# Scratch of q and k in DRAM by head pair, with loads split by head parity

## The chip, the cores and the metric

One NeuronCore of a Trainium2 chip runs the whole kernel. The metric is the device time of one execution in microseconds (us). Most executions of a kernel agree to 0.3%, some are 1 to 2% longer.

## The reference

Eight batches (B = 8) of causal attention with H = 8 heads of D = 64 over S = 576 tokens, each head with 16 extra "beacon" keys in front, then an MLP (512 to 2048 to 512, ELU) on all 4608 tokens:

```python
k_all = concat([beacon_k, k], axis=2); v_all = concat([beacon_v, v], axis=2)
scores = q @ k_all^T / sqrt(64), causal over k
attn = softmax(scores) @ v_all                # (8, 8, 576, 64)
x = attn.transpose(0, 2, 1, 3).reshape(4608, 512)
out = elu(x @ w_in) @ w_out                   # fp32
```

## The kernel before

TensorE needs q and k with d on the partitions. Batches 0 and 1 are transposed on TensorE. For batches 2 to 7, POOL (the GpSimd engine) issues loads that cast q and k from fp32 to bf16 into a DRAM scratch (four loads a tensor, each 144 tokens of all heads), and SP (SyncE) issues DMA transposes out of the scratch, two (q and k) for each head pair:

```python
    @step
    def ld(b, i, s0):                       # issued by POOL; i = 0: q, 1: k; s0 = 0, 144, 288, 432
        if (b, i) not in st:
            st[b, i] = dram.tile([S, H, D], BF16, tag=f"qk{i}", name="qkd")
        s1 = s0 + S // 4
        nc.gpsimd.dma_start(
            out=st[b, i][s0:s1], in_=(q, k)[i][b, :, s0:s1].rearrange("h s d -> s h d"))

    @step
    def ct(b, p):                           # issued by SP, one head pair p
        for i in range(2):
            nc.sync.dma_start_transpose(
                out=keys(b, p)[:, i, NB:SK], in_=st[b, i][:, 2 * p:2 * p + 2, :].rearrange("s h d -> s (h d)"))
    # ... cut: scores, exp, masks, sums, MLP
```

The order of all steps is a fixed list of words. A word "ld.3.0.144:a.1.3.3" is the load of batch 3, q, tokens from 144, held back ("gated") until the named step is done. The score matmuls S read `keys(b, p)`; TensorE's instructions stand in this order too, so a late transpose stops what is behind it (in the changed kernel once for 17.4 us).

The softmax here doesn't subtract the row's maximum and nothing guards it: scores larger than these inputs give would overflow.

## Time and profile before

| | before |
|---|---|
| time, median (range) | 344.25 us (343.25 to 348.1, 4 runs) |
| profiled execution | 342.8 us, granted TensorE clock 0.996 |
| TensorE busy / idle | 328.5 / 14.3 us |
| last load of batches 2 / 4 / 7 landed at | 54.6 / 106.9 / 187.5 us |
| median distance between landings of q/k loads | 1.5 us |

The main views are in the prediction below. Here are the lines of the transfers (DMA view of the kernel before: total packets; then tensors, issuing queue, count, KB each, median us from issue to landing):

```profile
DMA packets 137536, 35.97 MB, mean 105 GB/s; under 512 B 125712, under 2 KB 132880, under 8 KB 137488
...
qkd<-in_q_dram POOLq DMA_DIRECT2D x24, 144.0 KB, 5.7
qkd<-in_k_dram POOLq DMA_DIRECT2D x24, 144.0 KB, 5.6
...
qk<-qkd SPq DMA_TRANSPOSE x48, 4.9
```

and POOL's time on the loads (its groups of instructions: count | busy us, mean ns of one | idle before):

```profile
L174 POOL DMA_DIRECT2D qkd<-in_k_dram x24 | 22.0, 919 | 11.9 <-DVE ls L480 4.1 <-DVE et L378 2.8 <-DVE qk L282 2.2
```

At the median a load lands within 6 us, and a transpose takes 4.9 us.

### The profile page before, as it was taken

How to read it: one execution, taken by the hardware profiler on the slowest of the kernel's cores; microseconds unless marked ns; L12 is line 12 of the kernel's file. 1: busy time of each engine (PE TensorE's matmuls, PEld its weight loads, DVE VectorE, ACT ScalarE, POOL GpSimd, SP SyncE). 2: the span in 40 equal slices, each digit the busy share in tenths (PEclk: the TensorE clock that was granted, in tenths of full speed). 3: DMA queues.
4: the chain of work that ended last, by engine and by line, in shares of the span. 5: the costliest groups of instructions: out<-in, count | busy, mean ns of one | idle time of the engine just before them, and what ended most of it. 6: DMA issues, size and time to landing. Idle time of an engine off the chain costs nothing.

```text
span 342.8 us, 10834 instructions
## 1 busy us (share of the span) xinstructions
PE 328.5 (96%) x4694; PEld 187.0 (55%) x4694; DVE 252.0 (74%) x583; ACT 209.3 (61%) x250; POOL 98.2 (29%) x126
## 2 busy tenths in 40 slices
PE   7989999889999999999999999999999999999992
PEld 3656786355555555565555565555455555555551
DVE  1668599599999999788999987798876456783000
ACT  1988962788795876898796688735424225242111
POOL 7485456554174445342253001200000000000000
PEclk9999999999999999999999999999999999999998
DMA  8999999999999999999999644411000013003104
GB/s 127 159 152 184 205 173 148 140 144 110 174 113 147 119 218 129 149 145 112 167 123 106 105 143 29 32 13 65 0 2 2 0 63 122 3 2 122 63 0 185
DMA packets 137536, 35.97 MB, mean 105 GB/s; under 512 B 125712, under 2 KB 132880, under 8 KB 137488
## 3 DMA queue, kind: packets, MB, share of 16 engines
q0 software_dynamic: 102240, 18.49, 70.0%
q1 hardware_dynamic: 34528, 16.39, 24.1%
q8 instruction: 37, 0.61, 0.8%
q10 hardware_dynamic: 720, 0.39, 0.4%
q14 instruction: 11, 0.09, 0.1%
HBM read 37.22 MB, written 16.52 MB: 157 GB/s over the span
## 4 chain that ended last, share of the span: by engine, by line
PE 83%; DVE 6%; DMA 6%; ACT 2%; issue 1%; POOL 0%; SPq 0%; DVEq 0%; ACTq 0%; POOLq 0%
PE ops L601 35%; PE hps L560 32%; PE sc L325 6%; PE ut L391 4%; DVE gt L585 3%; DMA qk<-qkd 2%; DMA w_in<-in_moe_w_in_dram 2%; PE lt L391 2%; DVE gt L578 1%; PE lt L496 1%; PE tqk L274 1%; DMA stg<-in_q_dram 1%; DVE qk L293 1%; DMA out_dram<-osb 1%; PE ua L391 1%
## 5 line engine op out<-in xcount | busy, mean ns | idle before, releaser
L560 PE MATMUL hps<-xT,w_in 64*128 64x512 f16 (+1 forms) x1280 | 140.0, 355 | 2.4 <-DVE xT L451 1.2
L601 PE MATMUL ops<-w_out,gt 64*128 64x512 f16 x1152 | 138.2, 376 | 0.0
L362 ACT ACTIVATE et<-sc 128x1024 f16<-128x1024 f32 (+4 forms) x128 | 104.6, 867 | 21.9 <-PE sc L325 20.5
L573 ACT ACTIVATE e<-hps 128x1024 f32<-128x1024 f32 x72 | 73.2, 1023 | 62.6 <-PE hps L560 59.9
L560 PEld LDWEIGHTS <-w_in 64*128 64x128 f16 x1280 | 68.4, 94 | 52.7 <-issue 2.5
L601 PEld LDWEIGHTS <-gt 64*128 64x128 f16 x1152 | 62.9, 94 | 53.6 <-issue 0.3
L585 DVE TENSOR_TENSOR gt<-hps,gt 128x1024 f16<-128x1024 f32 x72 | 87.8, 1221 | 4.7 <-DVE gt L578 0.5
L578 DVE TENSOR_SCALAR gt<-e 128x1024 f16<-128x1024 f32 x72 | 49.8, 694 | 21.3 <-ACT e L573 21.0
L191 POOL DMA_DIRECT2D v<-in_v_dram x40 | 33.8, 849 | 62.7 <-DVE xT L451 22.6
L378 DVE TENSOR_TENSOR et<-et,triu 128x256 f16<-128x256 f16 (+6 forms) x185 | 38.0, 253 | 10.0 <-ACT et L362 9.9
L325 PE MATMUL sc<-qk 64*128 64x64 bf16 (+16 forms) x528 | 39.1, 247 | 1.6 <-DMA qk<-qkd 1.5
L325 PEld LDWEIGHTS <-qk 64*128 64x128 bf16 x528 | 23.1, 94 | 18.1 <-DMA qk<-qkd 2.2
L480 DVE TENSOR_TENSOR ls<-ls,et 128x672 f16<-128x672 f16 (+2 forms) x84 | 29.4, 366 | 0.6
L174 POOL DMA_DIRECT2D qkd<-in_q_dram x24 | 21.4, 899 | 27.2 <-DVE qk L282 9.7
L614 ACT COPY osb<-ops 128x1024 f32<-128x1024 f32 x11 | 11.1, 1011 | 25.1 <-PE ops L601 25.1
L391 PEld LDWEIGHTS <-v 128*32 128x32 f16 x1248 | 21.0, 96 | 8.1 <-issue 2.4
L174 POOL DMA_DIRECT2D qkd<-in_k_dram x24 | 22.0, 919 | 11.9 <-DVE ls L480 4.1
L451 DVE TENSOR_TENSOR xT<-ut,rl 128x448 f16<-128x448 f32 (+6 forms) x56 | 20.0, 413 | 2.9 <-PE ut L391 1.9
L391 PE MATMUL ut<-et,v 128*32 128x512 f16 (+4 forms) x560 | 19.0, 278 | 0.0
L630 DVE COPY osb<-ops 128x512 f32<-128x512 f32 x1 | 0.7, 692 | 24.6 <-PE ops L601 24.6
L480 DVE TENSOR_TENSOR ls<-et 128x928 f16<-128x928 f16 x28 | 17.5, 634 | 0.3
L525 ACT ACTIVATE rl<-lt 128x576 f32<-128x576 f32 x14 | 9.1, 653 | 9.3 <-PE lt L391 9.3
(47 smaller groups left out, 122.1 us busy)
## 6 DMA issues: line engine op xcount, KB each, us to landing
out_dram<-osb SPq DMA_DIRECT2D x17, 512.0 KB, 3.5
qkd<-in_q_dram POOLq DMA_DIRECT2D x24, 144.0 KB, 5.7
qkd<-in_k_dram POOLq DMA_DIRECT2D x24, 144.0 KB, 5.6
v<-in_v_dram POOLq DMA_DIRECT2D x24, 128.0 KB, 4.9
w_in<-in_moe_w_in_dram POOLq DMA_DIRECT2D x8, 256.0 KB, 8.5
w_out<-in_moe_w_out_dram POOLq DMA_DIRECT2D x4, 512.0 KB, 9.4
v<-in_v_dram POOLq DMA_DIRECT2D x8, 112.0 KB, 4.1
stg<-in_k_dram POOLq DMA_DIRECT2D x3, 288.0 KB, 5.9
```

The lines of the kernel that those rows point to most:

```text
L174: nc.gpsimd.dma_start(out=st[b, i][s0:s1], in_=(q, k)[i][b, :, s0:s1].rearrange("h s d -> s h d"))
L191: nc.gpsimd.dma_start(out=v_tile(b)[r0:r0 + n_, j, :, :], in_=v[b, :, ilo[j]:ilo[j] + n_, :].rearrange("h s d -> s h d"))
L325: nc.tensor.matmul(out=s[:, h, o0 + a - c0:o0 + e - c0], lhsT=t[D * h:D * (h + 1), 1, P * j:P * (j + 1)], rhs=t[D * h:D * (h + 1), 0, NB + ...
L362: nc.scalar.activation(out=ets[b, p][:, :, c0:c1], in_=s[:, :, o0:o0 + c1 - c0], func=AFT.Exp, bias=0.0, scale=SCALE)
L378: nc.vector.tensor_tensor(out=o, in0=o, in1=triu[0:kc[j], :, t0:t0 + e - a], op=ALU.mult)
L391: nc.tensor.matmul(out=t[32 * i:32 * (i + 1), a - qa:e - qa], lhsT=ones[0:kc[j], :] if half is None else v16[0:kc[j], j, h, half::2], rhs= ...
L480: nc.vector.tensor_tensor(out=lsum[b, p][0:kc[j], :, qj - q1:], in0=in0, in1=e_[0:kc[j], :, cj:cj + S - qj], op=ALU.add)
L560: both.append(nc.tensor.matmul(out=hp[t, i][:, out_, w * u:w * (u + 1)], lhsT=w_in16[rows, cc, P * fc:P * (fc + 1)], rhs=xt[k_][rows, cc, ...
L573: nc.scalar.activation(out=eb[t, i], in_=hp[t, i], func=AFT.Exp, bias=0.0, scale=1.0)
L578: nc.vector.tensor_scalar(out=rb[t, i], in0=eb[t, i], scalar1=1.0, scalar2=1.0, op0=ALU.min, op1=ALU.subtract)
L585: nc.vector.tensor_tensor(out=gt, in0=hp[t, i], in1=gt, op=ALU.max)
L601: both.append(nc.tensor.matmul(out=o_[out_][:, 0, :] if len(o_) == 2 else o_[0][:, out_, :], lhsT=gts[t, fc][rows, P * (2 * tp + out_):P * ...
```

## The change

Intent: in the old scratch a transpose reads 576 rows of 256 B, one every 1024 B. With the scratch laid out as [head pair, token, parity, d], it reads one contiguous block of 147 KB. A load of all heads would then need a pattern of four dimensions (pair, token, parity, d); to stay at three, each load takes 288 tokens of the four even or the four odd heads.

```diff
     def ld(b, i, s0):
         if (b, i) not in st:
-            st[b, i] = dram.tile([S, H, D], BF16, tag=f"qk{i}", name="qkd")
-        s1 = s0 + S // 4
+            st[b, i] = dram.tile([NP, S, 2, D], BF16, tag=f"qk{i}", name="qkd")
+        s0, e_ = s0 // (S // 2) * (S // 2), s0 // (S // 4) % 2
+        s1 = s0 + S // 2
         nc.gpsimd.dma_start(
-            out=st[b, i][s0:s1], in_=(q, k)[i][b, :, s0:s1].rearrange("h s d -> s h d"))
+            out=st[b, i][:, s0:s1, e_, :], in_=(q, k)[i][b].rearrange("(p e) s d -> p e s d", e=2)[:, e_, s0:s1, :])
 ...
     def ct(b, p):
         for i in range(2):
             nc.sync.dma_start_transpose(
-                out=keys(b, p)[:, i, NB:SK], in_=st[b, i][:, 2 * p:2 * p + 2, :].rearrange("s h d -> s (h d)"))
+                out=keys(b, p)[:, i, NB:SK], in_=st[b, i][p].rearrange("s e d -> s (e d)"))
```

## The prediction

> **What bounds the kernel now.** I read the busy totals first, then the slices, the waits, and last the timeline where a wait names the tiles that the change touches.
>
> ```profile
> span 342.8 us, 10834 instructions
> PE 328.5 (96%) x4694; PEld 187.0 (55%) x4694; DVE 252.0 (74%) x583; ACT 209.3 (61%) x250; POOL 98.2 (29%) x126
> ...
> PE   7989999889999999999999999999999999999992
> ...
> DMA  8999999999999999999999644411000013003104
> ...
> q0 software_dynamic: 102240, 18.49, 70.0%
> q1 hardware_dynamic: 34528, 16.39, 24.1%
> ```
>
> TensorE has work in 328.5 of 342.8 us; only 14.3 us of its time is idle, most of it in the first eighth. The DMA row is at 9 through slice 22 (to about 195 us), so transfers could also be a limit there. The waits of TensorE (its matmuls, PE, and its weight loads, PEld) from 55 us to the end say whether they are:
>
> ```profile
> PE sc L325 <- DMA qk<-qkd: 1.5, 2, 1.2
> PE hps L560 <- DVE xT L451: 1.2, 1, 1.2
> ...
> PEld L325 <- DMA qk<-qkd: 2.2, 2, 1.7
> ```
>
> The score matmuls (L325) waited for transposed q and k twice, 1.5 us in all on the matmul row. The timeline places both in batch 2, the first batch that takes the DRAM path:
>
> ```profile
> 60.72 0.39 PE L325 MATMUL sc<-qk 64*128 64x512 bf16 x2 [0.31 <-DMA qk<-qkd]
> ...
> 66.14 0.63 PE L325 MATMUL sc<-qk 64*128 64x144 bf16 x12 [1.19 <-DMA qk<-qkd]
> ```
>
> After that TensorE has no gap in most windows (22.00 busy of 22.00 us from 91 to 113, 28.00 of 28.00 from 169 to 197). So the kernel is TensorE-bound, and the q/k path costs 1.5 us today. What the change can win is at most about that; what it can lose is a q/k path that becomes late.
>
> How late may it become? For each batch I took from the trace when its eight loads landed (the 16th count of their semaphores), when the transposes landed, and when the first score matmul of that head pair started. The smallest distance from landing to use over the four pairs is: batch 2: 0.0 us (both waits above), batch 3: 1.8, batch 4: 2.4, batch 5: 3.4, batch 6: 4.8, batch 7: 3.6 us. A delay larger than this stalls TensorE by the excess.
>
> **What the Trainium skill says.** Three places of the page "DMA: Bandwidth & Descriptors" bear on it.
> (1) Section "Why a DMA increments its semaphore by 16 and not by 1": the number k of DMA engines that one transfer uses is the largest number up to 16 that divides the slowest dimension of both access patterns; a software-generated DMA with k below 16 takes k consecutive engines from a round-robin cursor. It also names an exception, in which some such DMAs are cut into ceil(rows/16) rows an engine. The kernel before has no DMA with k under 16 (outer sizes 1152/144, 128, 112, 96, 80, 16), so its trace can't confirm it.
> (2) Section "Why small descriptors are slow (HBM only)": a 256-byte descriptor takes 11 cycles of the DMA engine[...]: from 107 to 109 us the loads ran flat out with 2,418 packets of 128 B (256 B read as fp32), 16 x 2,000 / 2,418 = 13.2 ns each.
> (3) Section "Latency and other measured facts": a DMA transpose reaches 261 GB/s from a non-contiguous source and 350 to 400 from a contiguous one. In the trace a transpose (147 KB, 576 packets of 256 B) alone has its packets within about 1 us, 147 GB/s, and lands 2.7 to 2.9 us after its issue, so neither figure is reached.
>
> **The change part by part.** Instruction counts and order on all engines are unchanged: 48 loads on POOL, 48 transposes on SP, and TensorE, DVE and ACT see the same tiles. Two things change.
>
> Loads. Before, the destination is one run of 1152 rows of 128 B and the source is 144 x 8 rows: both outer sizes divide by 16, so 16 engines get 72 rows each. After, both patterns are 4 (head pairs) x 288 x 64; the slowest dimension is 4, so k = 4 and each engine gets 288 rows. Bytes and descriptors (1152) are the same. Alone, the stream takes 288 x 13.2 ns = 3.8 us in place of 72 x 13.2 = 0.95: a load lands 2.85 us later. The load issued at 91.9 us with empty queues landed at 95.8, 3.9 us; I expect about 6.7 for such a one. As the four consecutive engines rotate, four successive loads cover all 16, and the total work of an engine per batch (2 x 288 against 8 x 72 rows) is the same: throughput stays, latency grows. In a queue that is already backed up even the latency of the last load doesn't grow: an engine has then skipped the three loads between, and finishes the same 2 x 288 = 8 x 72 rows.
>
> That is the case in batch 2: its loads were issued from 24.3 to 48.0 us behind the weights, and the last landed at 54.6, 6.6 us after its issue. So I expect 0 to 1 us there, not 2.85. In batches 3 to 7 the last load was issued with a shorter queue and landed 4.1 to 6.4 us after issue; there I take the full 2.85 us. It passes through the transposes (the first k transpose of each of these batches is issued within 0.3 us of the last k load's landing when SP is free, as in batch 3: 80.9, 81.0) to the first uses.
>
> Transposes. The 576 rows of 256 B become one 147 KB block. TensorE sees only landing times. The skill's ratio, 261 to about 375, applied to the 1 us of packets gives an estimate of 0.3 us less; issue on SP (1.2 us each, median) and the completion stay. Under competing loads it may be more: the second transpose of pair 1 in batch 2 took 7.4 us to land.
>
> Sum on TensorE: batch 2: 0 to +1, less 0.3 to 0.6 of its 1.5 us of waits: about 0. Batch 3: 2.85 - 0.3 - 1.8 = +0.75. Batch 4: 2.85 - 0.3 - 2.4 = +0.15. Batches 5 to 7 have 3.4 us or more: 0. I add 0.5 for loads of v, which use all 16 engines and now end with the slowest group (they landed 15 us or more before use in batches 2 and 3). Total about +1.4 us on the 344.12 us median: **345.5 us**.
>
> **Rivals.**
> A. *The transposes become much faster and the batch-2 waits go.* For: the waits on qk are the only visible cost of this path. Against: they are 1.5 us on the matmul row. Time 342 to 343 us, still within 2%.
> B. *k = 16 stays* (the exception of (1), or a generator that cuts the inner dimension). Then only the transposes change: 343.5 to 344.
> C. *k = 4, but always on the same four engines* (the exception of (1) with one row on each of the first four). Then all 48 loads queue on four engines: 8 x 3.8 = 30 us a batch, plus their share of v (288 rows x 13.2 = 3.8) and of transposes (4608/16 x 13.2 = 3.8), 38 us a batch, where the loads of successive batches now follow at 23 to 31 us. From 24 us on, with about 10 us of weights in front, the last loads end near 24 + 10 + 6 x 38 = 262 us in place of 187.5, and what TensorE still has to do after batch 7's first use (146 us) comes after it: 400 to 425 us. Against: the page gives the rotating cursor as the general case. Nothing in the trace before excludes C. I give it 15%.
> D. *k = 4 rotating, but no backlog helps batch 2 and transposes gain nothing*: +2.85 + 1.05 + 0.45 = 4.4 us, 348.5, plus some for v: 350.
>
> **Range and chances.** A, B and the main line lie between 342 and 347, D at 348 to 350. The three runs before spread from 343.25 to 348.1 by themselves. 342 to 352 holds this, and leaves out C. Faster by 2% would need 6.9 us from a wait of 1.5: 0.02. Slower by 2% is C and a part of worse collisions: 0.19. Same: 0.79.
>
> **What would show it.** Right: loads of q and k land 2.5 to 3 us later after issue where queues are short (the median of 5.6 to 5.7 us becomes 7.5 to 9), the packets of a lone load run at about 300 per us in place of 1,200; transposes land a little sooner than 4.9 us; the waits of L325 for qk grow from 1.5 us to 2 to 4 us, in batches 2 to 4; TensorE's busy time stays near 328.5 us. Wrong: unchanged load landings (B); waits of 10 us and more for qk in every batch and loads landing tens of us after issue (C); or transposes that get slower, as the only new cost that I see no reason for.

## The result, and the profile after

Median 459.45 us (456.62 to 461.35, 4 runs), 33% slower: ratio 1.331, 95% interval 1.318 to 1.344. A ratio here is the mean time of one kernel's fast runs over that of the other's in the same rounds, so not quite the ratio of the medians quoted. The forecast of 342 to 352 us was wrong.

The same views of the changed kernel. Its page, busy totals, slices (PE, granted clock PEclk, DMA) and software queue:

```profile
span 456.4 us, 10834 instructions
...
PE 349.2 (77%) x4694; PEld 189.7 (42%) x4694; DVE 262.2 (57%) x583; ACT 210.6 (46%) x250; POOL 141.9 (31%) x126
...
PE   8887908588319914994299559809999999999994
...
PEclk9998967799859975998589859967999999999998
DMA  9999999999999999999999999965341000120213
...
DMA packets 303424, 36.63 MB, mean 80 GB/s; under 512 B 291600, under 2 KB 298768, under 8 KB 303376
...
q0 software_dynamic: 268128, 19.15, 87.1%
```

The instruction counts are the same to the last one, the span is 113.6 us longer. TensorE's idle time grew from 14.3 to 107.2 us and its busy time by 20.7 us; the clock row dips in and after the slices where it stood still (0.884 on average, 0.996 before), so I take most of the 20.7 for a result of the stops and not a cause. From slice 28 of the 40 on the PE row is as before.

What TensorE waited for (waits of the changed kernel: us in total, times, longest):

```profile
PEld L326 <- DMA qk<-qkd: 78.4, 9, 17.9
PE sc L326 <- DMA qk<-qkd: 73.8, 9, 17.4
...
PE ops L602 <- DMA w_out<-in_moe_w_out_dram: 12.5, 1, 12.5
```

1.5 us of waits for transposed q and k became 73.8, and w_out, a load that nobody touched, cost 12.5. Together 86.3 of the 92.9 us that TensorE's idle time grew. So the q/k path is late, and so is w_out, which shares its queue.

Why is it late? The transfers (DMA view of the changed kernel) and POOL's rows:

```profile
qkd<-in_q_dram POOLq DMA_DIRECT2D x24, 144.0 KB, 11.3
qkd<-in_k_dram POOLq DMA_DIRECT2D x24, 144.0 KB, 12.2
v<-in_v_dram POOLq DMA_DIRECT2D x24, 128.0 KB, 9.2
...
qk<-qkd SPq DMA_TRANSPOSE x48, 7.0
```

```profile
L175 POOL DMA_DIRECT2D qkd<-in_k_dram x24 | 43.7, 1820 | 55.1 <-DVE et L379 13.7 <-DVE gt L579 9.7 <-DVE qk L283 9.5
```

The loads land twice as late, and POOL spends 1.8 us on each in place of 0.9, for a transfer of the same bytes. The packet total says what happened: 303,424 in place of 137,536. (A descriptor is one piece of a transfer, as a DMA engine gets it; in these kernels the trace shows each as a packet.) By size, the software queue carried 93,184 packets of 128 B in both kernels, but 167,776 packets of 4 B in place of 1,888. The difference is 165,888 = 48 loads x 3,456, and 3,456 is 12 x 288: **each load works on four engines with 288 rows each, and the other twelve engines get a 4-byte filler for each of the 288 rows.** A load of 1152 descriptors became one of 4608.

Throughput fell with it: the median distance between landings went from 1.5 to 4.5 us; the last loads of batches 2, 4 and 7 landed at 77.0, 170.8 and 302.8 us (54.6, 106.9 and 187.5 before).

### The profile page after: what moved, and what is told of

It reads as the page before. It is cut to its first block, busy times and chain, and to the rows that moved or that the text cites. A ratio compares the mean times of both kernels' runs of the same rounds, so it can differ in the third digit from the quotient of the medians.

```text
span 456.4 us, 10834 instructions
## 1 busy us (share of the span) xinstructions
PE 349.2 (77%) x4694; PEld 189.7 (42%) x4694; DVE 262.2 (57%) x583; ACT 210.6 (46%) x250; POOL 141.9 (31%) x126
## 2 busy tenths in 40 slices
DMA packets 303424, 36.63 MB, mean 80 GB/s; under 512 B 291600, under 2 KB 298768, under 8 KB 303376
## 4 chain that ended last, share of the span: by engine, by line
PE 39%; DMA 23%; issue 16%; DVE 9%; POOL 8%; SPq 3%; ACT 1%; POOLq 0%; DVEq 0%; ACTq 0%
PE ops L602 19%; PE hps L561 15%; DMA qkd<-in_k_dram 10%; POOL qkd L175 6%; DMA qk<-qkd 5%; SPq L289 3%; DMA w_out<-in_moe_w_out_dram 3%; PE sc L326 2%; DVE gt L579 2%; DVE gt L586 2%; PE ut L392 2%; DVE et L379 2%; DVE ls L481 2%; DMA v<-in_v_dram 1%; DMA w_in<-in_moe_w_in_dram 1%
## 5 line engine op out<-in xcount | busy, mean ns | idle before, releaser
L602 PE MATMUL ops<-w_out,gt 64*128 64x512 f16 x1152 | 146.6, 393 | 12.5 <-DMA w_out<-in_moe_w_out_dram 12.5
L561 PE MATMUL hps<-xT,w_in 64*128 64x512 f16 (+1 forms) x1280 | 145.8, 365 | 4.7 <-DVE gt L586 2.0
L326 PE MATMUL sc<-qk 64*128 64x64 bf16 (+16 forms) x528 | 42.2, 261 | 74.5 <-DMA qk<-qkd 73.8
L602 PEld LDWEIGHTS <-gt 64*128 64x128 f16 x1152 | 63.9, 98 | 73.3 <-issue 23.6
L561 PEld LDWEIGHTS <-w_in 64*128 64x128 f16 x1280 | 69.7, 96 | 58.7 <-issue 10.1
L586 DVE TENSOR_TENSOR gt<-hps,gt 128x1024 f16<-128x1024 f32 x72 | 87.7, 1221 | 4.7 <-DVE gt L579 0.5
L579 DVE TENSOR_SCALAR gt<-e 128x1024 f16<-128x1024 f32 x72 | 58.6, 817 | 35.0 <-ACT e L574 34.9
L175 POOL DMA_DIRECT2D qkd<-in_q_dram x24 | 42.6, 1778 | 61.9 <-DVE et L379 19.1
L175 POOL DMA_DIRECT2D qkd<-in_k_dram x24 | 43.7, 1820 | 55.1 <-DVE et L379 13.7
```

Source lines behind the costliest of these rows:

```text
L175: nc.gpsimd.dma_start(out=st[b, i][:, s0:s1, e_, :], in_=(q, k)[i][b].rearrange("(p e) s d -> p e s d", e=2)[:, e_, s0:s1, :])
L326: nc.tensor.matmul(out=s[:, h, o0 + a - c0:o0 + e - c0], lhsT=t[D * h:D * (h + 1), 1, P * j:P * (j + 1)], rhs=t[D * h:D * (h + 1), 0, NB + ...
L561: both.append(nc.tensor.matmul(out=hp[t, i][:, out_, w * u:w * (u + 1)], lhsT=w_in16[rows, cc, P * fc:P * (fc + 1)], rhs=xt[k_][rows, cc, ...
L579: nc.vector.tensor_scalar(out=rb[t, i], in0=eb[t, i], scalar1=1.0, scalar2=1.0, op0=ALU.min, op1=ALU.subtract)
L586: nc.vector.tensor_tensor(out=gt, in0=hp[t, i], in1=gt, op=ALU.max)
L602: both.append(nc.tensor.matmul(out=o_[out_][:, 0, :] if len(o_) == 2 else o_[0][:, out_, :], lhsT=gts[t, fc][rows, P * (2 * tp + out_):P * ...
```

## The experiments

The first theory after the result was rival C of the prediction ("few engines"): that the data always sits on the same four engines. Its rivals were the layout itself and POOL's own time a load.

**e1: the new layout, tokens outermost in the loads.** The layout and the transposes of the change stay; only the order of the dimensions of the loads is turned.

```diff
-            out=st[b, i][:, s0:s1, e_, :], in_=(q, k)[i][b].rearrange("(p e) s d -> p e s d", e=2)[:, e_, s0:s1, :])
+            out=st[b, i][:, s0:s1, e_, :].rearrange("p s d -> s p d"),
+            in_=(q, k)[i][b].rearrange("(p e) s d -> s p e d", e=2)[s0:s1, :, e_, :])
```

> New layout and transposes kept, the loads' patterns turned to 288 x 4 x 64 (rows of s outermost). Few engines (a load whose slowest dimension is 4 puts its 1152 rows on the same four DMA engines and 4-byte fillers on the other twelve): 4-byte packets on the software queue fall from 167,776 to about 1,888, the load on POOL takes 0.89 us again, landing is 5 to 6 us, time 342 to 346 us. Layout to blame (two loads writing alternate 128-byte halves, or the contiguous transpose): the time stays above 400 us. Transposes: if a contiguous block helps, they land in under 4.9 us and the waits for qk in batch 2 (1.5 us before) shrink.

Measured: 346.48 us against 344.63 of before in the same rounds, ratio 1.0045 (1.0008 to 1.0081). DMA view and waits of e1:

```profile
DMA packets 137536, 35.97 MB, mean 104 GB/s; under 512 B 125712, under 2 KB 132880, under 8 KB 137488
...
qk<-qkd SPq DMA_TRANSPOSE x48, 5.0
```

```profile
PE sc L327 <- DMA qk<-qkd: 1.9, 2, 1.0
```

The fillers and the loss are gone with one reordered pattern that moves the same bytes to the same places. It also answers what the contiguous block is worth by itself: nothing in the time. Transposes land in 5.0 us (4.9 before), and their queue still carries 28,160 packets of 256 B, as before; 27,648 of them, 576 each, are the transposes'. Only those with the queues to themselves are a little quicker: 2.5 to 2.8 us in batch 7 of the changed kernel (median 2.6), 2.7 to 3.3 before (median 2.8). POOL's time a load was 1.06 us, not the 0.89 expected.

**e2: the old layout, the head pair outermost in the loads.** The counterpart: the old scratch and the strided transposes, with the change's order of dimensions in the loads alone.

```diff
-            out=st[b, i][s0:s1], in_=(q, k)[i][b, :, s0:s1].rearrange("h s d -> s h d"))
+            out=st[b, i][s0:s1].rearrange("s (p e) d -> p e s d", e=2)[:, e_],
+            in_=(q, k)[i][b].rearrange("(p e) s d -> p e s d", e=2)[:, e_, s0:s1, :])
```

> Old layout and strided transposes, the loads alone turned to 4 x 288 x 64 (head pair outermost, split by parity). Few engines: as slow as the change, 450 to 465 us, 167,776 four-byte packets, load on POOL 1.77 us. Layout or transposes to blame: about 344 us.

Measured: 457.23 us (455.0 to 461.86), ratio 1.324; the profiled execution was one of the longer ones. DMA view and waits of e2:

```profile
DMA packets 303424, 36.63 MB, mean 80 GB/s; under 512 B 291600, under 2 KB 298768, under 8 KB 303376
```

```profile
PE sc L327 <- DMA qk<-qkd: 78.8, 10, 19.5
```

The same packet count and the same loss as the change: all of it is in the order of the dimensions of the loads. Layout and transposes are acquitted.

**e3: old layout, heads outermost.** A smaller dose: slowest dimension 8.

```diff
-            out=st[b, i][s0:s1], in_=(q, k)[i][b, :, s0:s1].rearrange("h s d -> s h d"))
+            out=st[b, i][s0:s1].rearrange("s h d -> h s d"), in_=(q, k)[i][b, :, s0:s1])
```

> Old layout, quarters of s as before, but heads outermost: 8 x 144 x 64. Few engines: eight engines carry 144 rows each, 1.9 us a load; a batch is 8 x 1.9 = 15 us plus 7.6 us for v and transposes, 23 us on the loaded engines, less than the 27 us in which batches follow: 345 to 365 us; fillers 8 x 144 = 1,152 a load, about 57,000 four-byte packets in all. Rotating engines (a cursor): within 1% of before. If POOL's own time per load is the cause, then its load of about 1.2 us costs a third of the change's loss, 380 us.

Measured: 359.88 us, ratio 1.041 (1.035 to 1.047). Queue and waits of e3:

```profile
q0 software_dynamic: 157536, 18.71, 76.2%
```

```profile
PE sc L325 <- DMA qk<-qkd: 8.8, 5, 4.6
```

Fillers as forecast: 57,184 packets of 4 B, (57,184 - 1,888)/48 = 1,152 a load. The time lay in the range of "the same engines each time", and I read it so at first. That reading does not hold (see e5): with 8 engines and 2,304 descriptors a load both theories give a loss of this kind. POOL's own time as the cause should have given 380 us; POOL took 1.14 us a load.

**e4: like e1, with 296 and 280 tokens in place of 288 and 288.**

```diff
-        s0, e_ = s0 // (S // 2) * (S // 2), s0 // (S // 4) % 2
-        s1 = s0 + S // 2
+        s0, e_ = s0 // (S // 2), s0 // (S // 4) % 2
+        s0, s1 = ((0, 296), (296, S))[s0]
```

> As e1_s_outer, but 296 and 280 rows of s, which 16 does not divide (8 does). If rows are dealt as ceil(rows/16) an engine: 19 and 18 steps of rows on 16 engines, few fillers (32 and 32 a load, about 3,400 four-byte packets in all with the completions), time as e1 within 1%. If the engine count is the largest divisor up to 16, eight engines carry 148 rows of 128 B each and the time is that of e3_heads_outer.

Measured: 352.25 us, ratio 1.025 (1.019 to 1.031; at a threshold of 2% that is an unclear verdict), 34,144 packets of 4 B, (34,144 - 1,888)/48 = 672 a load on average. My expectation had slipped: 16 doesn't divide 280, but 14 does. With the largest divisor up to 16, 296 tokens give 8 engines and 8 idle ones x 148 fillers = 1,184; 280 give 14 engines and 2 x 80 = 160; the mean is 672, to the packet. Dealing out ceil(rows/16) would have given 32. So the divisor rule holds. Some 6 us above e1 (346.48 in the same rounds) is what the fewer engines and 672 fillers a load cost here. It also speaks against POOL's own time as the cause: POOL took 1.46 us a load here and 1.14 in e3, which was the slower kernel.

**e5 and its control e5c: bytes on four engines without many descriptors.** Good loads (e1), and ahead of each load one extra copy into scratch that nobody reads, of few large descriptors. In e5 its slowest dimension is 4, in e5c 16, for the same bytes.

```diff
+        dm = dram.tile([4, 6, 4160], BF16, tag=f"dm{b}_{i}_{s0}", bufs=1, name="dm")
+        nc.gpsimd.dma_start(
+            out=dm[:, 0:5, 0:4096],
+            in_=(q, k)[i][b].rearrange("(p e) s d -> p (e s d)", e=2)[:, 0:20480].rearrange("p (n c) -> p n c", n=5))
```

(e5c: `[16, 6, 1040]`, `[:, 0:5, 0:1024]`, and 16 rows of 5120 elements as the source.)

> e1_s_outer (good loads), and ahead of each of the 48 loads one extra copy of 320 KB (fp32 read, bf16 written to scratch that nobody uses) with pattern 4 x 5 x 4096: few and large descriptors (20 of 16 KB read), so hardly any fillers and hardly any generating on POOL, but all bytes on four engines, about 3.2 us each (80 KB at the 25.6 GB/s at which w_in's 2-KB reads went). Same four engines each time: a batch puts 8 x (3.2 + 0.95) + 7.6 = 41 us on them: 430 to 470 us, as bad as the change. Four engines that rotate, or descriptor generation as the cause of the change's loss: near its control e5c, 345 to 360 us.

> Control of e5: the same extra bytes and the same number of extra copies, with pattern 16 x 5 x 1024, on all engines, 0.8 us each. A batch: 8 x (0.8 + 0.95) + 7.6 = 21.6 us an engine, under the 27 us period: 347 to 358 us under every theory. If it is as slow as e5, the cost is in the number of DMAs (at most eight in flight, semaphores shared) and not in the engines.

Measured: e5 412.83 us, ratio 1.195; e5c 365.08 us, ratio 1.060, itself 7 us above the range that was expected under every theory. Waits of e5 (its profiled execution was one of the longer ones), then of e5c:

```profile
PE sc L331 <- DMA qk<-qkd: 48.7, 10, 10.8
```

```profile
PE sc L331 <- DMA qk<-qkd: 14.2, 9, 3.0
```

e5 fits neither expectation: 48 us above its control, but well below the 430 to 470 of "the same four". The packet records decide it. A packet of the extra copy takes about 625 ns, and the records come in chains that fit engines running them one after the other (starts at 111.02 and 111.64 us; the trace doesn't name the engines). On four fixed engines about four could then be in flight, but in the trace up to 16 were. So **the group of four moves on from one DMA to the next**. The changed kernel shows it too: its 128-byte packets reached 157 in 0.25 us (at 133.2 us, with no load of v in flight), twice the 77 at which four engines run flat out. "The same four engines", my first theory and rival C, falls. What e5 does show is that bunching costs by itself. A likely reason, not shown, is that a transfer whose share lies on four engines makes later DMAs, which need all 16, wait for the slowest group. A rival remains: e5's rows are four times as long as its control's (16 KB read against 4), and the transposes landed in 7.7 us against 5.4. The extra copy itself also got its share of fillers, (5,536 - 2,656)/48 = 60 = 12 x 5 a copy (2,656 are the completions of all 166 DMAs), too few to matter.

**e6: as many extra descriptors as the change has fillers, spread evenly.** One extra copy of 3456 single fp32 elements ahead of each good load.

```diff
+        dm = dram.tile([3456, 2], FP32, tag=f"dm{b}_{i}_{s0}", bufs=1, name="dm")
+        nc.gpsimd.dma_start(
+            out=dm[:, 0:1],
+            in_=(q, k)[i][b].rearrange("h s d -> (h s d)")[0:6912].rearrange("(n t) -> n t", t=2)[:, 0:1])
```

> e1_s_outer, and ahead of each load one extra copy of 3456 single fp32 elements on all 16 engines: as many extra descriptors as the change has fillers (12 x 288), without any concentration of data. Engines as the cause: 216 x 7 to 9 ns = 1.5 to 1.9 us more on each engine a load, 8 x (0.95 + 1.7) + 7.6 = 29 us a batch against a period of 27: 350 to 375 us. Descriptor generation on POOL as the cause (4608 descriptors a load in place of 1152, about 4 us): as slow as the change, 430 to 470 us.

Measured: 756.94 us, ratio 2.194, far outside both. The trace records 64 such elements as one packet of 256 B, median 81 ns but 307 on average, and doesn't show where the rest of the time went. The run separates nothing.

**e7: the change without the 48 gates.**

```diff
-    ... ld.3.0.0:V.1.0.1 ...
+    ... ld.3.0.0 ...            # and so for all 48 words
```

> The change, with the 48 manual gates that hold a q/k load back until a named DVE step taken away (buffer dependences stay). If the part of the loss above the serial estimate of 400 to 425 us is the loop in which late scores delay the DVE steps that let the next loads go, the time falls to 400 to 440 us. If the loads are limited by the engines all the time, it stays within 2% of 459 us.

Measured: 453.33 us, ratio 1.314. POOL's waits before the loads (waits of e7):

```profile
POOL qkd L175 <- issue: 87.7, 27, 10.5
```

The landings follow each other as before (median 4.4 us apart, 4.5 in the change). POOL now stands before its loads for 87.7 us (13.3 in the change) with nothing in the profile that it waits for; I take that for a full queue. So the loop through the gates is not the cause. The run leaves the v loads on POOL, which still wait 66 us in all, nearly all of it for DVE steps.

**e8 and e9: engine time or number of descriptors?** Both are e1 plus an extra copy ahead of each load, evenly on 16 engines: e8 with 640 KB in 160 descriptors, e9 with 3456 rows of 64 B.

```diff
+        dm = dram.tile([16, 11, 1040], BF16, ...)         # e8
+            out=dm[:, 0:10, 0:1024], in_= ... 16 rows of 10240 elements
+        dm = dram.tile([3456, 64], BF16, ...)             # e9
+            out=dm[:, 0:32], in_=(q, k)[i][b].rearrange("h s d -> (h s) d")[0:3456, 0:32])
```

> As e5c, but 640 KB in each extra copy (16 x 10 x 1024): about 1.6 us more on every engine a load, with 160 descriptors only. By packet times the change's fillers and data cost an average engine less than that: (3.8 + 3 x 1.9)/4 - 0.95 = 1.4 us a load. If engine time is what the change lacks, this is as slow as the change (459 us) or slower; if it is the making of 4608 descriptors a load, this stays well below: 8 x (0.95 + 1.6) + 7.6 = 28 us a batch, 375 to 405 us.

> e6 done better: ahead of each good load one extra copy of 3456 rows of 64 B (128 B read), slowest dimension 3456, so all 16 engines, no fillers and no concentration; 216 rows an engine at an estimated 8 ns = 1.8 us, like e8. Descriptors made per load and extra copy: 4608, as in the change. Descriptor making as the cause: 430 to 480 us, far above e8. Engine time as the cause: within 5% of e8.

Measured: e8 404.78 us, ratio 1.168; e9 440.13 us, ratio 1.270. Waits of e8, then of e9:

```profile
PE sc L331 <- DMA qk<-qkd: 36.8, 11, 9.7
```

```profile
PE sc L331 <- DMA qk<-qkd: 61.4, 9, 13.0
```

e9's small rows ran at up to 1,900 a us where a backlog had built up, 8.4 ns each on 16 engines, so 216 of them are 1.8 us an engine: near e8's 1.6 us (an estimate: 10 rows an engine, each a quarter of e5's 625 ns). Yet e9 is 35 us slower, 8.7%, though it moves two thirds of e8's extra bytes (432 KB read a copy against 640); and with no filler and no bunching it comes within 20 us of the change. That speaks for the number of descriptors, with the reserve that 8.4 ns is the pace of bursts only. But e8, at the upper end of its range, shows that engine time costs as well: with only 160 descriptors more a load it lost 59 us against before (345.98 in these rounds), half of the change's loss.

**e10: four engines, half the descriptors.** The change with rows of 256 B. The rows mix tokens and heads of a pair. Its output is wrong, which doesn't matter for the time. (The comparison with the reference still passed its tolerance, which says nothing for the kernel.)

```diff
+        h_, t_ = s0 // (S // 2), s0 // (S // 4) % 2
+            out=st[b, i].rearrange("p (h r t) e d -> p h r t (e d)", h=2, t=2)[:, h_, :, t_, :],
+            in_=(q, k)[i][b].rearrange("(p e) s d -> p (e s d)", e=2).rearrange(
+                "p (h r t c) -> p h r t c", h=2, t=2, c=2 * D)[:, h_, :, t_, :])
```

> The change with its slowest dimension of 4 kept (four data engines, twelve with fillers), but rows of 256 B in place of 128 B: 4 x 144 x 128, so 576 data descriptors and 1,728 fillers a load, 2,304 in place of 4,608, for the same bytes. The rows mix heads and tokens: the result is wrong on purpose. Data on four engines as the cause: 144 x 22 ns = 3.2 us a load in place of 3.8, 420 to 450 us. Number of descriptors as the cause: as e3_heads_outer, which also makes 2,304 a load: 350 to 370 us.

Measured: 388.54 us (383.39 to 392.8), ratio 1.114. Queue and waits of e10:

```profile
q0 software_dynamic: 157536, 18.82, 75.6%
```

```profile
PE sc L327 <- DMA qk<-qkd: 25.7, 9, 5.9
```

Between the two expectations. (The 22 ns a row came out: 44 packets of 256 B in 0.25 us is the commonest count, 22.7 ns on each of four engines.) Same bytes, same groups of four, half the descriptors: 70.9 of the 115.2 us lost came back (459.45 - 388.54 against 459.45 - 344.25). e3, with the same 157,536 packets on the queue but its data on eight engines, is 29 us faster still. So both count: more than half of the loss goes with the number of descriptors, and with it the time that engines spend on them, which e10 halves too; bunching is the likely rest.

| kernel | descriptors made a load | engines with q/k data | median us between landings | time, us |
|---|---|---|---|---|
| before | 1152 | 16 | 1.5 | 344.25 |
| e3 | 2304 | 8 | 2.1 | 359.88 |
| e10 | 2304 | 4 | 2.5 | 388.54 |
| e9 | 4608 with its copy | 16 | 3.7 | 440.13 |
| the change | 4608 | 4 | 4.5 | 459.45 |

Except in the kernel before, where loads are issued no faster than they land, the landings follow at 0.9 to 1.2 descriptors a ns whatever the engines: 2304/2.1 = 1.1, 2304/2.5 = 0.9, 4608/3.7 = 1.2, 4608/4.5 = 1.0. That holds for runs that add descriptors; in e8, which adds bytes, 1312 descriptors came 3.0 us apart.

No version found here beats the kernel before; e1 comes closest, at 1.0045.

## Why the prediction was wrong, step by step

- *TensorE-bound, the q/k path costs 1.5 us today, and a delay beyond 0 to 4.8 us stalls TensorE.* Right, and the loss arose just there: 73.8 us of waits of the score matmuls. The slack was read well; the delay was not. Two side readings slipped without consequence: of the 14.3 us idle only 4.7 lie in the first eighth (6.3 lie in the last 9 us), and slice 22 ends at 188.5 us, not 195.
- *k = 4, 288 rows an engine, groups that rotate.* Right: 12 x 288 fillers a load, and the overlaps in the packet records.
- *A lone load lands about 6.7 us after issue, with packets at about 300 a us.* Nearly right: the load issued at 270.6 us, with empty queues, landed after 7.3 us; four engines showed 77 packets in 0.25 us. (The 13.2 ns were read from 107 to 109 us, when loads of v ran, the last load of q and k having landed at 106.9. Batch 2 has 1,210 packets in 1 us at 45.5, the same pace.)
- ***"Bytes and descriptors (1152) are the same", hence "throughput stays, latency grows".*** This is the step that failed. The bytes are the same; the descriptors are 4608, because the twelve engines without data get 288 fillers each. Landings came 4.5 us apart in place of 1.5. Eight loads then need 8 x 4.5 = 36 us, and v comes on top, where batches used to follow at 24 to 31 us; from batch to batch the last load landed 40 to 50 us apart.
- *In a queue that is backed up, the last load of batch 2 doesn't get later (0 to 1 us).* Wrong for the same reason: 77.0 us in place of 54.6. The backlog argument counted only data rows an engine, 2 x 288 = 8 x 72; an engine also worked through 6 x 288 fillers.
- *Batches 3 to 7: 2.85 us later each.* Mis-sized: the last loads landed 46 us (batch 3) to 115 us (batch 7) later, because the delay adds up from batch to batch when throughput is short. A fixed latency would have been paid once against the slack.
- *Transposes 0.3 us sooner.* About 0.2 us where they run alone, nothing in the median (5.0 us in e1), nothing in the time. In the changed kernel they landed in 7.0 us, the sign for which the prediction saw no reason. As e1 has the same transposes at 5.0 and e2 the old ones at 7.0, that comes from the loads and not from the layout.
- *v costs 0.5 us.* v loads landed in 9.2 us in place of 4.9 and w_out alone stopped TensorE for 12.5 us: the untouched loads sit in the same software queue.
- *Rival C, 400 to 425 us at 15%.* The nearest number from the wrong mechanism, so near by luck. C's four fixed engines were refuted in e5; the sum, 8 x 3.8 us a batch, looked alike because 4608 descriptors at about 1.1 a ns take about as long as 288 rows of 13.2 ns. A fit of the total would have confirmed the wrong cause.
- *Rival B, k = 16.* Refuted by the packet count.

What stays open is where the descriptors cost their time. In the lone load at 270.6 us an idle engine got some 36 fillers in 0.5 us (427 to 449 on twelve engines). One takes 9 ns in the records (median), so some 55 would fit, and 1,033 in 0.5 us, 65 on each of 16 engines, were seen at 219.8 us, after a backlog; the data engines were below their pace, too, for the first 2 us. That looks as if engines waited for descriptors. Whether POOL makes them no faster, or the engines hold each other up, or work on other engines holds POOL up, no run here tells, as each run that raised the count also raised the engines' load.

## What to carry to other kernels

Put a dimension that 16 divides outermost on both sides of a DMA, and check the packet count before and after: when bytes stay and 4-byte packets appear, idle engines are being fed. Reordering the dimensions of one access pattern was worth 33% here, while the contiguity that the change was made for was worth nothing. And in a queue that is nearly full, ask first whether a change touches throughput: latency is paid once against the slack, throughput again in each batch.

## What the Trainium skill lacked or had wrong

- "DMA: Bandwidth & Descriptors", "Why a DMA increments its semaphore by 16 and not by 1": the divisor rule holds (the fillers fit 8 engines for 296 rows and 14 for 280), and the group does move on (e5). That it moves as the page says was not checked. It says that on the software path all 16 engines post their count, but not that the engines without data get a 4-byte packet for every row step of the others: 3,456 a load with four engines, 1,152 with eight, 160 with fourteen. Its exception (ceil(rows/16) rows an engine) didn't apply to these DRAM-to-DRAM casts.
- Same page, "Anatomy of one DMA", where descriptor generation counts as "small, variable": with 2,304 to 4,608 descriptors a load, landings followed at 0.9 to 1.2 descriptors a ns, 4.5 us a load in the change. Whether the making took that time stays open.
- Same page, "Latency and other measured facts": 261 GB/s from a non-contiguous and 350 to 400 from a contiguous source for DMA transposes. Here both read packets of 256 B and landed in 4.9 and 5.0 us; alone, the contiguous ones were about 0.2 us sooner.
- No page has the price of single 4-byte elements on the software path: 48 copies of 3456 of them added 410 us (e6 against e1).
